# Transposing two steps in 64x64 tiles, and new instruction orders on every engine, in a fused attention and gated-MLP kernel

## The chip, the cores and the metric

The kernel runs on one core of a Trainium2 chip. The metric is device time in microseconds (us) from launch to end. The profile shows one execution: its span runs from the first to the last instruction of the program, and a little launch work lies around it.

## What is computed

Linear attention with a decay, block by block, for 4 batches, 8 heads, 768 tokens and 64 features, then a gated MLP over its output, read as 4 x 768 x 512:

```python
for b in range(nb):                                   # blocks of 64 tokens
    intra = einsum('bhic,bhjc->bhij', qb, kb) * Dmask # lam**(i-j) where i >= j
    intra = einsum('bhij,bhjd->bhid', intra, vb)
    inter = einsum('bhid,bhde->bhie', qb * lam_pow, kv_state)
    out[:, :, sl] = intra + inter
    kv_state = lam**block * kv_state + einsum('bhsd,bhse->bhde', kb * rev_pow, vb)

h = maximum(x @ w_in, 0); u, v = h[..., :512], h[..., 512:]
v_n = (v - mean(v)) / sqrt(var(v) + 1e-6)
v_s = einsum('ts,bsd->btd', w_spatial, v_n) + b_spatial[None, :, None]
return (u * v_s) @ w_out
```

## The kernel before

The tokens are worked in 12 steps of 256, three to a batch (step n belongs to batch n // 3). A step takes this way, with the name of each operation in the order table in brackets:

1. Three loads of 512 KB for q, k, v (LQ, LK, LV), each into one of three buffers, on SyncE's DMA queue (SP).
2. k times a power of lam (KM, two halves), q converted (QC) or multiplied (QM), v converted (VC), all to bf16.
3. k and q transposed. Steps 0 to 2 do it on TensorE (PE) in halves of four 128x128 transposes (TK, TQ), steps 3 and 4 with eight for k and eight for q, each set into a PSUM bank of its own; EK copies k out and EQ multiplies q by a power of lam (table `lq`, built by LT) on its way out. Steps 5 to 11 leave the transposing to the DMA (DK, DQ) and scale q before it (QM).
4. Scores (SC, 16 matmuls of 64x64 tiles, L347), masked on VectorE into `a_sb` (MK, 128x1024, L352), running state (KV, L364; KS mixes it with half the scores, L377 and L385; SS copies it out), the attention output (AV, L406 and L415), copied out as `xT` (EX).
5. The MLP's first matmuls: the v half (PV, L440) and the u half (PU, L488) with ReLU (EV, EU), statistics of v (BN, RA, RD, NB) and normalising (VN).

Once a batch's three steps are through, the spatial matmul (PW, L514, with the bias laid into PSUM before it by GP), the gate (GM), the output matmul (PO, L525; the last tile in two halves, PH, L534), its copy (EO) and the store (ST) follow, while later batches go through 1 to 5. `w_spatial` is transposed on PE first (WT, L500). The weights come by GpSimd's DMA queue, with a cast: `w_in` in two halves (WI.0 is v's, WI.1 is u's), `w_spatial` in two (WS), `w_out` (WO). GT is a 1x1 copy on GpSimd (POOL) that holds its queue until a load has landed. FN is the like on PSUM, FL four idle matmuls.

Nothing is scheduled by a planner at build time. The table `ORDER` names every operation, its step, half and PSUM banks, and the engine that runs it (last letter: T TensorE, D VectorE (DVE), A ScalarE (ACT), P GpSimd, S SyncE), and each engine runs its operations in the table's order, waiting by semaphores for its inputs and for the buffers and PSUM banks that it overwrites:

```python
for token in ORDER.split():
    name, *args, e = token.split(".")
    ops[name](e, *map(int, args))
```

Of the kernel before, what the change touches and what calls it, by code (L numbers as in the profile page):

```python
# [21 lines left out]
FL.4.6.T MK.0.0.2.3.D TQ.2.0.2.T MK.1.1.0.1.D AV.0.0.3.6.T FN.0.3.6.A TQ.2.1.0.T SS.0.1.A MK.1.0.4.5.D LT.2.A
KM.2.0.P KV.1.0.T AV.1.0.1.4.T KM.2.1.D WS.1.P TK.2.0.5.T AV.0.1.3.6.T LV.2.S SS.1.0.D FN.1.1.4.A KV.1.1.T
LK.3.S EX.0.1.6.A AV.1.1.1.4.T BS.S LK.5.S EX.1.0.1.A EK.2.0.5.D LQ.3.S EX.0.0.3.D PV.0.1.5.T FL.15.6.T
EX.1.1.4.A WO.P TK.2.1.3.T GT.1.2.P PV.1.1.1.T EV.1.1.1.A EQ.2.1.0.D EQ.2.0.2.D VC.2.P WT.0.0.0.T EK.2.1.3.D
SC.2.0.2.3.T PV.1.0.4.T BN.1.1.D PV.0.0.6.T EW.0.0.0.A MK.2.0.2.3.D EV.0.1.5.A EV.1.0.4.A SC.2.1.0.1.T SS.1.1.A
PU.1.1.5.T BN.1.0.D WT.2.0.4.T KV.2.0.T MK.2.1.0.1.D RA.1.A BN.0.1.D LV.3.S AV.2.0.2.3.T EV.0.0.6.D SS.2.0.A
FN.2.2.3.D PU.1.0.0.T BN.0.0.D AV.2.1.2.3.T EX.2.1.3.D RD.1.D WT.1.0.1.T RA.0.A NB.1.D RD.0.D EX.2.0.2.A
EW.1.0.1.D EW.2.0.4.A NB.0.D VN.0.0.A WT.1.1.6.T GT.2.1.P KM.3.0.P EW.1.1.6.D KM.3.1.P GT.2.2.P VC.3.P
WT.2.1.3.T EW.2.1.3.D PV.2.1.2.T PV.2.0.1.T VN.1.0.A PU.2.1.4.T EU.1.0.0.A VN.0.1.D LK.4.S LQ.4.S KM.4.1.P  # L30
KM.4.0.P EV.2.0.1.A QC.4.2.P PU.0.0.6.T LV.4.S PU.0.1.3.T LQ.5.S WT.0.1.0.T LV.5.S LK.6.S VN.1.1.A PU.2.0.1.T
EU.1.1.5.A EV.2.1.2.D BN.2.1.D BN.2.0.D RA.2.A RD.2.D EU.0.0.6.A GP.0.2.1.2.A EW.0.1.0.D VN.2.1.D GP.0.0.0.5.A
VN.2.0.D EU.0.1.3.A QC.3.2.D LQ.6.S GP.0.1.1.6.A EU.2.0.1.D TK.3.2.0.T PW.0.0.0.5.T GM.0.0.0.5.D EU.2.1.4.D
GP.0.2.0.3.A PW.0.2.0.3.T TQ.3.2.1.T EQ.3.2.1.D GM.0.2.0.3.D EK.3.2.0.A PW.0.2.1.2.T SC.3.1.4.5.T MK.3.1.4.5.D
KS.3.0.0.1.T SS.3.0.A GP.0.0.1.3.A PW.0.1.1.6.T GP.0.3.1.4.A KS.3.1.0.1.T KM.5.1.P KM.5.0.P DK.5.S GM.0.2.1.2.D
MK.3.0.0.1.D TK.4.2.5.T EK.4.2.5.A PW.0.0.1.3.T PW.0.3.1.4.T GP.0.1.0.2.A GM.0.1.1.6.D GP.0.3.0.0.D AV.3.0.1.5.T
# [551 lines left out]
```

## Time and profile before

| | before |
|---|---|
| median of 3 runs | 147.1 us (146.69 to 147.25) |
| the profiled execution | 147.07 us |
| its span | 145.4 us |
| PE busy | 131.9 us, 91% of the span |
| DVE, ACT, POOL busy | 113.0, 76.2, 53.7 us |
| DMA | 32.28 MB, 222 GB/s on the mean |

A busy PE is not one at its peak: matmuls are pipelined and the ends in the profile are modelled, so the distance from one group's start to the next one's tells more than the busy time. The rows quoted in the prediction give for each group its start and its length in us, and, in square brackets, how long its engine sat idle before it and what ended that.

### The profile page before, as it was taken

To read this page: it belongs to the slowest core of one execution; us is meant where nothing else is said; L and a number is where in the kernel's file an instruction comes from. 1 tells how busy PE (TensorE), PEld (TensorE's weight loads), DVE (VectorE), ACT (ScalarE), POOL (GpSimd) and SP (SyncE) were. 2 spreads that over 40 slices of the span, in tenths; PEclk is the share of its full clock that TensorE was granted. 3 is DMA by queue.
4 is the path that set the end of the run, shared out by engine and by line. 5 is a ranking of instruction groups with operands and counts; after the bars stand their busy time and mean duration, and the time that the engine had idled before them with its cause. 6 is when DMAs were issued, how large, how long until landed. Compare 5 with 4: busy or idle time off the path is not lost.

```text
span 145.4 us, 4626 instructions
## 1 busy us (share of the span) xinstructions
PE 131.9 (91%) x1954; PEld 83.2 (57%) x1954; DVE 113.0 (78%) x229; ACT 76.2 (52%) x155; POOL 53.7 (37%) x66
## 2 busy tenths in 40 slices
PE   1169989799999999999999999999999999999980
PEld 1047755578756565468565645775566556665540
DVE  2568985988898888979989889878988798972720
ACT  3775276669834224299942444594341447880250
POOL 7439920305089637672825729234000000000000
PEclk9999999999999999999999999999999999999998
DMA  3999999999999999999997998999490700082064
GB/s 83 347 347 347 229 214 216 216 230 341 302 307 301 293 118 272 239 253 333 194 312 194 284 304 194 343 207 194 147 338 19 281 12 0 5 326 107 0 265 170
DMA packets 58375, 32.28 MB, mean 222 GB/s; under 512 B 15858, under 2 KB 55282, under 8 KB 58354
## 3 DMA queue, kind: packets, MB, share of 16 engines
q1 hardware_dynamic: 55968, 29.23, 77.8%
q0 software_dynamic: 2384, 2.75, 10.8%
q8 instruction: 15, 0.25, 0.7%
q14 instruction: 6, 0.05, 0.3%
q10 hardware_dynamic: 2, 0.00, 0.0%
HBM read 24.77 MB, written 6.29 MB: 214 GB/s over the span
## 4 chain that ended last, share of the span: by engine, by line
PE 77%; DMA 12%; SPq 5%; POOL 2%; DVE 1%; issue 0%; POOLq 0%
PE ps L514 21%; PE ps L488 15%; PE ps L525 14%; PE ps L440 12%; DMA win_sb<-in_moe_w_in_dram 8%; SPq L192 5%; DMA q_in<-in_q_dram 4%; PE ps L415 3%; PE ps L406 2%; PE ps L347 2%; PE ps L316 1%; POOL kc L286 1%; PE ps L500 1%; PE ps L385 1%; PE ps L377 1%; PE ps L534 1%
## 5 line engine op out<-in xcount | busy, mean ns | idle before, releaser
L514 PE MATMUL ps<-wt_sb,vn 128*128 128x384 bf16 x192 | 34.3, 326 | 0.0
L352 DVE TENSOR_TENSOR a_sb<-ps,m 128x1024 bf16<-128x1024 f32 x24 | 28.7, 1217 | 4.3 <-PE ps L347 1.8
L286 POOL TENSOR_TENSOR kc<-k_in,lv 128x512 bf16<-128x512 f32 x20 | 20.5, 1042 | 25.0 <-DMA k_in<-in_k_dram 15.8
L488 PE MATMUL ps<-xT,win_sb 128*128 128x256 bf16 x192 | 24.0, 273 | 0.8 <-DMA win_sb<-in_moe_w_in_dram 0.8
L514 PEld LDWEIGHTS <-vn 128*128 128x128 bf16 x192 | 17.9, 98 | 11.6
L440 PE MATMUL ps<-win_sb,xT 128*128 128x512 bf16 x96 | 23.6, 380 | 0.1
L525 PE MATMUL ps<-wout_sb,gT 128*128 128x512 bf16 x92 | 22.7, 380 | 0.0
L488 PEld LDWEIGHTS <-win_sb 128*128 128x128 bf16 x192 | 18.3, 98 | 5.8 <-DMA win_sb<-in_moe_w_in_dram 1.0
L520 DVE TENSOR_TENSOR gT<-ps,uT 128x384 bf16<-128x384 f32 x32 | 16.9, 548 | 4.7 <-PE ps L514 4.6
L455 DVE BATCH_NORM_STATS2 st<-vh 128x6 f32<-128x512 bf16 x24 | 16.3, 681 | 1.5 <-ACT vh L445 1.3
L177 ACT ACTIVATE o_sb<-ps 128x512 f32<-128x512 f32 (+1 forms) x19 | 10.8, 580 | 12.1 <-PE ps L525 12.1
L445 ACT ACTIVATE vh<-ps 128x512 bf16<-128x512 f32 x17 | 10.0, 596 | 13.1 <-PE ps L440 10.7
L177 ACT ACTIVATE xT<-ps 128x512 bf16<-128x512 f32 x15 | 8.6, 596 | 14.2 <-PE ps L415 14.2
L181 POOL CAST vb<-v_in 128x1024 bf16<-128x1024 f32 x9 | 9.3, 1037 | 15.2 <-DMA v_in<-in_v_dram 11.3
L286 POOL TENSOR_TENSOR qc<-q_in,lqn 128x512 bf16<-128x512 f32 x12 | 12.5, 1049 | 4.5 <-DMA q_in<-in_q_dram 4.4
L440 PEld LDWEIGHTS <-xT 128*128 128x128 bf16 x96 | 8.6, 98 | 9.0 <-ACT xT L177 0.3
L525 PEld LDWEIGHTS <-gT 128*128 128x128 bf16 x92 | 8.5, 98 | 8.3
L177 ACT ACTIVATE ps<-bsp 128x384 f32<-128x384 f32 x21 | 10.0, 492 | 3.2 <-DVE a_sb L352 1.9
L415 PE MATMUL ps<-a_sb,vb 64*64 64x128 bf16 x384 | 10.2, 221 | 0.3 <-issue 0.3
L476 ACT ACTIVATE vn<-vh,shift,rstd 128x512 bf16<-128x512 bf16 x12 | 9.3, 806 | 0.2 <-DVE shift L470 0.2
L445 ACT ACTIVATE uT<-ps 128x512 bf16<-128x512 f32 x15 | 8.8, 590 | 1.0 <-PE ps L488 0.9
L347 PE MATMUL ps<-qT,kT 64*64 64x128 bf16 x288 | 7.9, 238 | 0.9 <-ACT kT L177 0.5
(76 smaller groups left out, 170.9 us busy)
## 6 DMA issues: line engine op xcount, KB each, us to landing
q_in<-in_q_dram SPq DMA_DIRECT2D x12, 512.0 KB, 6.2
k_in<-in_k_dram SPq DMA_DIRECT2D x12, 512.0 KB, 6.2
v_in<-in_v_dram SPq DMA_DIRECT2D x12, 512.0 KB, 6.0
out_dram<-o_sb SPq DMA_DIRECT2D x23, 256.0 KB, 2.9
wsp_raw<-in_moe_w_spatial_dram POOLq DMA_DIRECT2D x2, 576.0 KB, 12.4
win_sb<-in_moe_w_in_dram POOLq DMA_DIRECT2D x2, 512.0 KB, 10.6
wout_sb<-in_moe_w_out_dram POOLq DMA_DIRECT2D x1, 512.0 KB, 17.3
bsp<-in_moe_b_spatial_dram SPq DMA_DIRECT2D x1, 384.0 KB, 21.0
```

What stands on the lines that cost most here:

```text
L177: nc.scalar.activation(out=o, in_=i, func=AF.Copy)
L286: vec(e).tensor_tensor(out=dst[n % NCA][:, u].rearrange("p u m o d -> p o (u m) d"), in0=src[n % NIN].rearrange("p (o u) m d -> p o u m d" ...
L347: nc.tensor.matmul(out=pa[o][row(c), w, j], lhsT=kT[n % NTR][row(o), u, j, c * Q64:(c + 1) * Q64], rhs=qv(n, o, u, c), start=(w == 0 and j ...
L352: nc.vector.tensor_tensor(out=a_sb[n % NA][:, i].rearrange("p o w j x -> p o w (j x)"), in0=ps[:, b0:b1 + 1:b1 - b0].rearrange("p o (w y) ...
L415: nc.tensor.matmul(out=po[c ^ o][row(w), c, i], lhsT=vb[n % NCA][row(c), 4 * o + u, j, :], rhs=a[row(c), i, o, w, j, :], start=(r == 0 and ...
L440: nc.tensor.matmul(out=bank(b), lhsT=x[:, slot(c, g)], rhs=win_sb[:, g, DH:DFF], start=(g == 0), stop=(g == NCH - 1))
L445: nc.scalar.activation(out=o, in_=i, func=AF.Relu)
L455: nc.vector.bn_stats(out=st6[p2][:, t], in_=vh[p2][:, t])
L488: nc.tensor.matmul(out=pu[:, f2].rearrange("p (c x) -> p c x", c=2), lhsT=win_sb[:, g, f * P:(f + 1) * P], rhs=x[:, slot(0, g):slot(1, g) ...
L514: nc.tensor.matmul(out=bank(b)[:, 0:HW], lhsT=vn[bb % 2][:, s, f * P:(f + 1) * P], rhs=wt_sb[:, s, i * HW:(i + 1) * HW], start=False, stop ...
L520: nc.vector.tensor_tensor(out=gT[bb % 2][:, f, cols], in0=bank(b)[:, 0:HW], in1=uT[bb % 2][:, f, cols], op=ALU.mult)
L525: nc.tensor.matmul(out=bank(b), lhsT=gT[bb % 2][:, f, t * P:(t + 1) * P], rhs=wout_sb[:, f, :], start=(f == 0), stop=(f == NCH - 1))
```

## The change

Two things. First, steps 3 and 4 get operations of their own: TT transposes k and q together, in 128 transposes of 64x64 in place of sixteen of 128x128. Token half c goes to one of two neighbouring PSUM banks, k to the lower and q to the upper half of each bank, and FK and FQ evict k and q across the two banks at once (FK where EK was, FQ with the multiplication of EQ). Second, the whole table `ORDER` is another one: the order on every engine, the engine that some operations run on, and the PSUM banks. Counted over the table, PE's matmul operations are the same but for the two steps' transposes. Among the operations that change engine, POOL gives two casts of v to ACT and DVE and takes two multiplications of q over from DVE; DVE also hands four conversions of q and four bias copies to ACT and takes three normalisations from it.

```diff
-LQ.0.S lam.A msk.P idn.P LK.0.S LQ.1.S mkc.D QC.0.1.D posk.P pos.P LB.0.T LN.0.A LL.D QC.0.0.P LK.1.S LX.A
+lam.A LQ.1.S QC.1.0.A QC.1.1.A LK.1.S posk.P pos.P LK.0.S LQ.0.S msk.P mkc.D GT.1.1.P idn.P LB.0.T LN.0.A
...
+    def pair(b0, b1, k):
+        return ps[:, b0:b1 + 1:b1 - b0].bitcast(BF16)[:, :, 512 * k:512 * k + 512].rearrange("p c (f y) -> p c f y", y=Q64)
+
+    def both(t):
+        return t.rearrange("p u m (c y) -> p c (u m) y", c=2)
+
+    def t_t(e, n, b0, b1):
+        for k, src in enumerate((kc, qc)):
+            bk = [bank(b).bitcast(BF16)[:, 512 * k:512 * k + 512].rearrange("p (u m y) -> p u m y", u=4, m=2) for b in (b0, b1)]
+            for u in range(4):
+                for m in range(2):
+                    for o in range(2):
+                        for c in range(2):
+                            nc.tensor.transpose(out=bk[c][row(o), u, m], in_=src[n % NCA][row(c), u, m, o],
+                                                identity=ident[row(c), row(c)])
+
+    def f_k(e, n, b0, b1):
+        copy(e, both(kT[n % NTR]), pair(b0, b1, 0))
+
+    def f_q(e, n, b0, b1):
+        nc.vector.tensor_tensor(out=both(qT[n % NTR]), in0=pair(b0, b1, 1), in1=both(lq[:, n % NR]), op=ALU.mult)
...
-               SC=s_c, MK=m_k, KV=k_v, KS=k_s, SS=s_s, ...
+               SC=s_c, MK=m_k, KV=k_v, TT=t_t, FK=f_k, FQ=f_q, KS=k_s, SS=s_s, ...
```

Three places of the new orders follow. On ACT, at the start, before: `loglam` is the logarithm of lam (LN), `lqn` and `lv` are the powers for q and k (LX), `lq` the table for q after the transpose (LT).

```order
1 L196 DMA lam_in_62<-in_lam_dram 1x8
2 L210 ACT_TABLE_LOAD
3 L210 ACTIVATE loglam_64<-ps_61 128x8
4 L219 ACT_TABLE_LOAD
5 L219 ACTIVATE lqn_74<-lv_73 128x48
6 L220 ACTIVATE lv_73<-lv_73 128x48
7 L224 ACTIVATE lq_75<-posq_71,llrow_65 128x256 x8
8 L177 ACTIVATE kT_0_100<-ps_61 128x512
9 L177 ACTIVATE vb_0_98<-v_in_0_91 128x1024
```

The same place after:

```order
1 L196 DMA lam_in_62<-in_lam_dram 1x8
2 L177 ACT_TABLE_LOAD
3 L177 ACTIVATE qc_1_97<-q_in_1_86 128x2x4x64 x2
4 L210 ACT_TABLE_LOAD
5 L210 ACTIVATE loglam_64<-ps_61 128x8
6 L219 ACT_TABLE_LOAD
7 L219 ACTIVATE lqn_74<-lv_73 128x48
8 L220 ACTIVATE lv_73<-lv_73 128x48
9 L224 ACTIVATE lq_75<-posq_71,llrow_65 128x256 x4
10 L177 ACTIVATE kT_1_101<-ps_61 128x512
11 L177 ACTIVATE qc_0_96<-q_in_0_85 128x2x4x64
12 L224 ACTIVATE lq_75<-posq_71,llrow_65 128x256 x4
```

Two conversions of step 1's q now stand ahead of the logarithm, and a third table load with them; the second four `lq` pieces, which step 0 needs, stand last, behind a copy of k and another conversion.

On DVE, before, from the first mask multiplication on (`a_sb`); `xT` is the input of the first MLP matmuls:

```order
15 L352 TENSOR_TENSOR a_sb_0_104<-ps_61,m01_68 128x1024
16 L179 COPY kT_1_101<-ps_61 128x512
17 L179 CAST qc_0_96<-q_in_2_87 128x2x4x64
18 L330 TENSOR_TENSOR qT_1_103<-ps_61,lq_75 128x512
19 L352 TENSOR_TENSOR a_sb_0_104<-ps_61,m01_68 128x1024
20 L352 TENSOR_TENSOR a_sb_1_105<-ps_61,m01_68 128x1024 x2
21 L286 TENSOR_TENSOR kc_0_94<-k_in_2_90,lv_73 128x2x4x64
22 L179 CAST s_sb_2_108<-ps_61 128x256
23 L179 COPY kT_0_100<-ps_61 128x512
24 L179 CAST xT_0_110<-ps_61 128x4x128
```

The same place after (L374 is the mask multiplication there):

```order
12 L374 TENSOR_TENSOR a_sb_0_104<-ps_61,m01_68 128x1024
13 L330 TENSOR_TENSOR qT_1_103<-ps_61,lq_75 128x512 x2
14 L374 TENSOR_TENSOR a_sb_0_104<-ps_61,m01_68 128x1024
15 L374 TENSOR_TENSOR a_sb_1_105<-ps_61,m01_68 128x1024
16 L286 TENSOR_TENSOR kc_0_94<-k_in_2_90,lv_73 128x2x4x64
17 L374 TENSOR_TENSOR a_sb_1_105<-ps_61,m01_68 128x1024
18 L179 CAST xT_0_110<-ps_61 128x4x128
19 L330 TENSOR_TENSOR qT_0_102<-ps_61,lq_75 128x512
20 L179 CAST vb_0_98<-v_in_2_93 128x1024
21 L179 COPY kT_0_100<-ps_61 128x512
22 L330 TENSOR_TENSOR qT_0_102<-ps_61,lq_75 128x512
23 L179 CAST xT_1_111<-ps_61 128x4x128
```

The four masks of steps 0 and 1 are still the bulk; more of step 2's work (`qT_0`, `kT_0`, `vb_0`) now comes ahead of the `xT` that the first MLP matmul takes (step 1's, in row 23).

On POOL, before, the weight loads (DMA rows) among the first conversions:

```order
15 L181 CAST qc_0_96<-q_in_0_85 128x2x4x64
16 L286 TENSOR_TENSOR kc_1_95<-k_in_1_89,lv_73 128x2x4x64
17 L248 DMA win_sb_79<-in_moe_w_in_dram 128x4x512
18 L181 CAST qc_1_97<-q_in_1_86 128x2x4x64
19 L253 DMA wsp_raw_81<-in_moe_w_spatial_dram 128x3x768
20 L181 CAST vb_1_99<-v_in_1_92 128x1024
21 L244 COPY seen_76<-q_in_1_86 1x1
22 L181 CAST qc_0_96<-q_in_2_87 128x2x4x64
23 L248 DMA win_sb_79<-in_moe_w_in_dram 128x4x512
```

The same place after:

```order
16 L181 CAST qc_0_96<-q_in_0_85 128x2x4x64
17 L181 CAST vb_0_98<-v_in_0_91 128x1024
18 L181 CAST qc_0_96<-q_in_2_87 128x2x4x64
19 L248 DMA win_sb_79<-in_moe_w_in_dram 128x4x512
20 L181 CAST vb_1_99<-v_in_1_92 128x1024
21 L286 TENSOR_TENSOR kc_0_94<-k_in_2_90,lv_73 128x2x4x64
22 L253 DMA wsp_raw_81<-in_moe_w_spatial_dram 128x3x768
23 L248 DMA win_sb_79<-in_moe_w_in_dram 128x4x512
24 L286 TENSOR_TENSOR kc_1_95<-k_in_0_88,lv_73 128x2x4x64
```

Both halves of `w_in` now stand behind conversions of later loads (of the sixth load, q of step 2, and of the ninth, k of step 2). `w_out`, which stood three rows further down (row 26), now stands behind the second multiplication of q for step 5, ten rows further down (row 34). SyncE's queue now begins with q and k of step 1, k and q of step 0, v of step 0, q and v of step 2, v of step 1, k of step 2.

More of the change, by code (lines that the diff above doesn't have):

```diff
@@ L22 @@
[L22 to L36, printed above, removed]
@@ L82 @@
+PW.3.1.0.1.T GM.3.1.1.3.D GM.3.0.0.6.D GM.3.2.1.5.D PW.3.3.1.2.T GM.3.3.1.2.D PW.3.3.0.4.T GM.3.1.0.1.D ST.2.5.S
+PO.3.3.0.T EO.3.3.0.A ST.1.2.S PO.3.4.3.T ST.2.1.S ST.2.4.S GM.3.3.0.4.D PO.3.2.6.T EO.3.4.3.A ST.3.4.S ST.3.3.S
+EO.3.2.6.A ST.3.2.S PO.3.1.5.T EO.3.1.5.A ST.3.1.S PO.3.0.2.T EO.3.0.2.A ST.3.0.S PH.3.5.1.1.T PH.3.5.0.4.T
+EH.3.5.1.1.A SH.3.5.1.S EH.3.5.0.4.D SH.3.5.0.S
 """
```

111 lines of the change are left out of this document (61 added, 50 removed).

## The prediction

> **What bounds the kernel now.** I read the page first, then the chain that ended last, then PE's waits after 25 us.
>
> ```profile
> span 145.4 us, 4626 instructions
> PE   1169989799999999999999999999999999999980
> 14.98 11.98 DMA win_sb<-in_moe_w_in_dram
> 27.00 1.05 PE ps L488 x8
> 141.34 0.43 DVE o_sb L179
> PE ps L488 <- DMA win_sb<-in_moe_w_in_dram: 0.8, 1, 0.8
> PE ps L316 <- POOL kc L286: 0.4, 1, 0.4
> ```
>
> The second row is PE's busy share in 40 slices: it fills within some 14 us and stays at 9 to the end. The chain's rows give start and length: the second half of `w_in` lands at 14.98 + 11.98 = 26.96 us, PE takes it at 27.00, and from there PE's work follows on itself to 141.34, where the last copy and the store begin. The last two rows are all that PE waited for after 25 us. So the time is when PE reaches its dense stretch, plus its work from there, plus the gaps in it. An operation on another engine counts only where it moves one of these three. The profiled execution took 147.07 us, 1.67 beyond its span and 0.03 under the median, so I add to 147.07. About 0.5% (0.7 us) is what a measurement of this kernel can tell from no change.
>
> **The start.** Here the new order does most. ACT's timeline of before, then DVE's:
>
> ```profile
> 1.34 1.28 ACT L210 ACT_TABLE_LOAD   x1 [1.34 <-PEq L572]
> 3.56 0.18 ACT L210 ACTIVATE loglam<-ps 128x8 f32<-128x8 f32 x1 [0.94 <-PE ps L207]
> 3.76 1.28 ACT L219 ACT_TABLE_LOAD   x1
> 6.22 0.24 ACT L220 ACTIVATE lv<-lv 128x48 f32<-128x48 f32 x1
> 6.37 3.28 ACT L224 ACTIVATE lq<-posq,llrow 128x256 bf16<-128x256 f32 x8
> 9.56 0.57 ACT L177 ACTIVATE kT<-ps 128x512 bf16<-128x512 bf16 x1
> 11.01 1.06 ACT L177 ACTIVATE vb<-v_in 128x1024 bf16<-128x1024 f32 x1 [0.87 <-DMA v_in<-in_v_dram]
> ...
> 4.96 0.43 DVE L179 CAST qc<-q_in 128x512 bf16<-128x512 f32 x1 [2.08 <-DMA q_in<-in_q_dram]
> 6.52 0.69 DVE L286 TENSOR_TENSOR kc<-k_in,lv 128x512 bf16<-128x512 f32 x1 [0.35 <-ACT lv L220]
> 9.69 0.42 DVE L330 TENSOR_TENSOR qT<-ps,lq 128x512 bf16<-128x512 bf16 x1 [0.64 <-ACT lq L224]
> 11.82 0.41 DVE L330 TENSOR_TENSOR qT<-ps,lq 128x512 bf16<-128x512 bf16 x1
> 12.15 1.21 DVE L352 TENSOR_TENSOR a_sb<-ps,m 128x1024 bf16<-128x1024 f32 x1
> 14.93 3.49 DVE L352 TENSOR_TENSOR a_sb<-ps,m 128x1024 bf16<-128x1024 f32 x3
> 18.34 0.68 DVE L286 TENSOR_TENSOR kc<-k_in,lv 128x512 bf16<-128x512 f32 x1
> 20.35 0.69 DVE L179 CAST xT<-ps 128x512 bf16<-128x512 f32 x1 [0.56 <-PE ps L415]
> 20.96 0.74 DVE L330 TENSOR_TENSOR qT<-ps,lq 128x512 bf16<-128x512 bf16 x2
> ```
>
> In before both table loads of 1.28 us lie under other waits, the power table `lv` is there at 6.46, `lq` ends at 9.65, and the first mask starts at 12.15. After, ACT first converts step 1's q, which lands where before's first load did, at 4.95. The row for 1024 elements has 1.06, that for 256 has 0.41 from one to the next (3.28 over eight), so I take 0.60 for 512. ACT then goes: two conversions to 6.15; the logarithm's table load, no longer under a wait, to 7.43; the logarithm to 7.6; the load for the powers to 8.9; `lqn` and `lv` to 9.4, against 6.46. Step 1's `lq` (four pieces, 1.6) to 11.0, a kT copy 0.5, a conversion 0.6, step 0's `lq` 1.6: to 13.7, against 9.65. DVE has multiplied its four k halves by then and waits. Then two qT and one kT (0.33 each, from 11.82 to 12.15) to 14.7, and the first mask starts at **14.85, 2.7 us later** than before.
>
> From there DVE's list decides. Up to the xT for the first v matmul it has four masks at 1.14 (14.93 to 18.34 is three), four qT and a kT at 0.33, two xT and a v conversion at 0.61 (20.35 to 20.96), one k half at 0.6: 4.56 + 1.65 + 1.83 + 0.6 = 8.6, done at 23.5. In before the first v matmul comes at 20.96. But its list left 1.5 us of step 2's conversions for later, and PE then still stood 0.8 for `w_in`, so I carry the sum to the first u matmul, before's 27.00. After, PE does more ahead of it: KV of step 2, both AV of step 2, two WT and one PV:
>
> ```profile
> 20.96 1.04 PE L440 MATMUL ps<-win_sb,xT 128*128 128x512 bf16 x4
> 27.00 1.05 PE L488 MATMUL ps<-xT,win_sb 128*128 128x256 bf16 x8 [0.80 <-DMA win_sb<-in_moe_w_in_dram]
> ...
> 30.07 0.24 PE ps L406 x8
> 30.31 0.22 PE ps L415 x16
> 30.53 0.78 PE ps L500 x12
> 31.81 1.73 PE ps L440 x8
> ...
> 23.97 0.69 DVE L455 BATCH_NORM_STATS2 st<-vh 128x6 f32<-128x512 bf16 x1 [1.07 <-ACT vh L445]
> 24.80 1.19 DVE L352 TENSOR_TENSOR a_sb<-ps,m 128x1024 bf16<-128x1024 f32 x1
> ```
>
> By these rows an AV is 0.46, two WT 0.78, a PV 0.87, and a KV 0.2 (sixteen at 14 ns, below): 2.8 together, so before's equal point is 29.8. After, DVE goes on from 23.5 with a mask (1.14), an xT (0.61), a statistics pair (0.83, from 23.97 to 24.80) once PV's ReLU is through at 25.4, and a mask, to 27.4. PE then does both AV and the four idle matmuls to 28.6, three WT to 29.7 while the last xT is copied, and PV to 30.6. The first u matmul starts at 30.6, **+0.8**. It is at least about 0, where `w_in` would hold PE (below), and up to +1.2 with each of the six masks at the 1.21 of a single one. I take +1.0, between the sum and that end, since the sum lets hand-overs between engines cost nothing.
>
> **The weights.** POOL's rows and the page's row of the landing times:
>
> ```profile
> 10.63 0.93 POOL L248 DMA_DIRECT2D win_sb<-in_moe_w_in_dram  x1
> win_sb<-in_moe_w_in_dram POOLq DMA_DIRECT2D x2, 512.0 KB, 10.6
> 14.13 0.43 DVE L179 CAST qc<-q_in 128x512 bf16<-128x512 f32 x1 [0.44 <-DMA q_in<-in_q_dram]
> ```
>
> 10.6 is the middle of two, and one is 11.98, so the first half took 9.2 and landed at 19.8. After, its issue stands behind the conversion of the sixth load. The fifth landed at 11.0 (ACT's `vb` row), the seventh at 14.0, so the sixth at 12.5, the issue comes at 13.3, the landing at 22.5: in time for 23.5. The second half landed 7.1 after the first, so 29.6: in time for 30.6, by 1.0. `w_out` leaves late. POOL's second multiplication for step 5 overwrites the buffer that step 3's q is transposed from, so it waits for TT.3 (37 us by the sum above) and the issue comes at about 40.5. With the 9.2 of `w_in`'s first half it lands at 49.7, just where the first PO stands (after five more PW, TT.4 and two tile groups from 41.5). Between 0 and 1.0 of waiting; I take +0.4.
>
> **The transposes.** PE rows of a 128x128 set and of 64x64 groups:
>
> ```profile
> 39.65 0.61 PE L316 MATMUL ps<-ident,qc 128*128 128x128 bf16 x8
> 40.10 1.14 PE L514 MATMUL ps<-wt_sb,vn 128*128 128x384 bf16 x6
> 55.89 0.41 PE L364 MATMUL ps<-vb,kc 64*64 64x64 bf16 x16
> 56.38 0.64 PE L347 MATMUL ps<-qT,kT 64*64 64x128 bf16 x32
> ```
>
> A set of eight takes 0.45 from its start to the next group's, so a step's k and q 0.90. No row shows a 64x64 transpose. The nearest is L364: 64 columns moved, sixteen in 0.41 less one's own 0.19, over fifteen, 14 ns each, with two of the four tiles in use at a time. TT uses all four in turn. If four run at once as L347's do (twice the columns in the same 14 ns), 128 take 0.93; if each costs 14 ns whatever runs beside it, 1.8. I take 1.0, by L347. That is +0.1 for each of two steps, up to +0.9. Changes between 64x64 groups and full ones are as many as before, 26 from the first PW on by the two orders, so TT adds none. The evictions have the elements of before.
>
> **The dense stretch.** The matmuls are the same. Before has two gaps from PW on: ahead of step 4's k (the 0.4 that L316 waits for POOL, in the first fence) and ahead of 56.38, where the last of L364's sixteen starts at 55.89 + 0.22 = 56.11 and the score matmuls 0.27 later. I let both go, -0.7, since TT.4 now stands behind AV of step 3 and DVE hands work over. In a new order of 139 PE groups something else will be late: I put 0.5 back, an estimate by those two gaps, of 0 to 2.
>
> Sum: 147.07 + 1.0 (start) + 0.2 (TT) + 0.4 (`w_out`) - 0.7 + 0.5 (gaps) = **148.5**.
>
> **Rivals.** *The start is absorbed* (not slower). If ACT's chain is at least 0.8 shorter (the 1.28 of the table load that stands ahead of the logarithm is the one piece that a different placing could take out whole), DVE's first mask starts before 14.05, PE is ready for the u matmul before 29.6, and `w_in`'s landing decides, as in before. Then the start costs nothing, and with the gaps closed and `w_out` in time the time is 147.07 + 0.2 - 0.7 = 146.6, and 146.1 where `w_in` lands 0.5 earlier than my sum as well. For it: in before PE had time to spare there, 0.8 at `w_in`. Against it: the order puts the table load where nothing covers it. *Transposes one after another*: if tiles don't overlap in a transpose, each is half of the 56 ns of a 128-column one, 28 ns, 3.6 us a step; 147.07 + 1.0 + 5.4 + 0.2 (the other terms) = 153.7. The L364 row speaks against it. The Trainium skill ("TensorE: Matmul & The Clock Gate", Part 1) says that start-to-start never drops below about 25 ns however few the columns; by it a step would take 3.2 us, an estimate. The 14 ns of L364 and L347 in this trace are already below that floor. At 14 ns each, the milder form, the time is 148.5 + 1.6 = 150.1. *A cold PE clock*:
>
> ```profile
> 11.29 1.03 PE L316 MATMUL ps<-ident,kc 128*128 128x128 bf16 x8
> 18.93 0.40 PE L316 MATMUL ps<-ident,kc 128*128 128x128 bf16 x4
> ```
>
> Eight transposes took 1.03 at 11.29 against 0.61 at 39.65, and four took 0.40 at 18.93, so PE ran at half pace at first and at the full one by then. After, it waits for masks between 16.5 and 18 and again before 23.5; if it comes to the PVs at half pace, two of them (0.87 each at the full pace) cost 1.7 more: 150.2. The Trainium skill (the same page, "The HAM clock gate") says that the clock is released after a window of about 3.4 us of sustained work, free-running; the dense 18 to 22.5 of my sum would hold such a window, so by that rule the clock is up in time.
>
> **How the numbers follow.** Forecast case (147.6 to 149.3) 0.47; start absorbed 0.25; TT at 14 ns 0.08, one after another 0.02; cold clock 0.10; gaps or `w_out` at their upper ends (149.3 to 150.6) 0.08. A fifth of the forecast case, 0.09, lies below 147.8. Of the absorbed case 0.12 falls below 146.4 and 0.13 above it. So faster 0.12, same 0.22, slower 0.66. The range leaves out 153.7, the top of the late cases and the lowest part of the absorbed one: 146.2 to 150.3.
>
> **What would show it.** The first mask at 14 to 15 us with a third table load ahead of the logarithm at 6.2; the first v matmul at 23 to 24, the first u matmul at 30 to 31 without a wait for `w_in`; TT at 0.9 to 1.1 us to the next group; PE gaps after 40 us under 1 us together. It is wrong if the first u matmul waits for `w_in` or starts before 30, if TT takes over 1.5, or if PE shows more than 2 us of gaps from PW on.

## The result, and the profile after

The changed kernel takes 148.63 us (median of 5 runs, 148.27 to 149.37), the kernel before 147.10 beside it (146.68 to 147.80): ratio 1.0115, 95% interval 1.0069 to 1.0162. It is slower by 1.2%, clear of the noise, and the forecast was 148.5. Ratios here and below leave out slow runs, those over 1.5% above the fastest of the same kernel, and the medians don't (three of e4's six runs are slow, and one each of e9's and e11's twelve). The profiled execution took 148.52 us, 1.45 more than that of before.

The page of after: span, PE's busy share and the granted clock in 40 slices of 3.67 us.

```profile
span 146.8 us, 4817 instructions
PE   0318599999999999999999999999999999999990
PEclk9999956999999999999999999999999999999999
```

PE fills later than in before, and the granted clock (the share of PE's full clock that the chip gave it) is halved around 18 to 25 us. ACT's timeline, then DVE's:

```profile
4.72 1.15 ACT L177 ACTIVATE qc<-q_in 128x512 bf16<-128x512 f32 x2 [2.10 <-DMA q_in<-in_q_dram]
5.89 1.28 ACT L210 ACT_TABLE_LOAD   x1
7.38 1.28 ACT L219 ACT_TABLE_LOAD   x1
8.95 0.24 ACT L220 ACTIVATE lv<-lv 128x48 f32<-128x48 f32 x1
...
15.11 1.22 DVE L374 TENSOR_TENSOR a_sb<-ps,m 128x1024 bf16<-128x1024 f32 x1
20.40 1.23 DVE L374 TENSOR_TENSOR a_sb<-ps,m 128x1024 bf16<-128x1024 f32 x1 [0.55 <-PE ps L369]
22.47 0.68 DVE L179 CAST vb<-v_in 128x1024 bf16<-128x1024 f32 x1
23.82 0.42 DVE L330 TENSOR_TENSOR qT<-ps,lq 128x512 bf16<-128x512 bf16 x1 [0.33 <-PE ps L316]
24.60 0.69 DVE L179 CAST xT<-ps 128x512 bf16<-128x512 f32 x1 [0.35 <-PE ps L437]
```

The third table load is there, ahead of the logarithm and under nothing. The power table is ready at 9.19 against 6.46, the first mask starts at 15.11 against 12.15. Between it and the `xT` for the first v matmul DVE stands three times, each time for PE. PE's timeline:

```profile
18.18 0.64 PE L437 MATMUL ps<-a_sb,vb 64*64 64x128 bf16 x16 [1.04 <-DVE a_sb L374]
25.35 1.90 PE L462 MATMUL ps<-win_sb,xT 128*128 128x512 bf16 x8 [0.22 <-DVE xT L179]
32.49 1.92 PE L510 MATMUL ps<-xT,win_sb 128*128 128x256 bf16 x16
38.11 0.45 PE L347 MATMUL ps<-ident,kc 64*64 64x64 bf16 x32
38.39 0.43 PE L347 MATMUL ps<-ident,qc 64*64 64x64 bf16 x32
38.76 1.92 PE L510 MATMUL ps<-xT,win_sb 128*128 128x256 bf16 x16
40.51 1.79 PE L536 MATMUL ps<-wt_sb,vn 128*128 128x384 bf16 x10
```

The first u matmul stands at 32.49, against before's equal point of 29.8: +2.7. The first w_spatial matmul stands at 40.51. Before's is at 37.65 with 0.45 of step 3's transposes still to come, so its equal point is 38.1: +2.4. PE's waits after 25 us and the last row of the chain:

```profile
PE ps L437 <- DVE a_sb L374: 0.2, 1, 0.2
PE ps L462 <- DVE xT L179: 0.2, 1, 0.2
143.25 0.42 DVE o_sb L179
```

The last copy starts at 143.25 against 141.34: +1.9, so the stretch from the first w_spatial matmul on became 0.5 shorter. From there to the end of the span it is 3.55 against 4.03, another 0.5 back. In sum +2.7 (start), -0.3 (to the first w_spatial matmul), -0.5 (dense stretch), -0.5 (tail): 1.4 of the 1.45.

### The profile page after: what moved, and what is told of

Read it like the earlier page. It is cut to its first block, busy times and chain, and to the rows that moved or that the text cites. A ratio compares the mean times of both kernels' runs of the same rounds, so it can differ in the third digit from the quotient of the medians.

```text
span 146.8 us, 4817 instructions
## 1 busy us (share of the span) xinstructions
PE 131.4 (89%) x2050; PEld 83.2 (57%) x2050; DVE 108.6 (74%) x217; ACT 82.5 (56%) x166; POOL 52.5 (36%) x65
## 4 chain that ended last, share of the span: by engine, by line
PE 57%; DMA 12%; DVE 8%; ACT 6%; SPq 5%; POOL 4%; issue 3%; POOLq 0%; DVEq 0%
PE ps L536 12%; PE ps L462 11%; PE ps L547 11%; PE ps L510 8%; DMA k_in<-in_k_dram 5%; DMA v_in<-in_v_dram 5%; PE ps L437 4%; DVE a_sb L374 3%; POOL qc L286 3%; PE ps L316 3%; DMA q_in<-in_q_dram 3%; PE ps L428 2%; DVE kc L286 2%; SPq L303 2%; SPq L192 2%
## 5 line engine op out<-in xcount | busy, mean ns | idle before, releaser
L536 PE MATMUL ps<-wt_sb,vn 128*128 128x384 bf16 x192 | 34.8, 326 | 0.1
L374 DVE TENSOR_TENSOR a_sb<-ps,m 128x1024 bf16<-128x1024 f32 x24 | 28.7, 1217 | 2.6 <-PE ps L399 1.2
L286 POOL TENSOR_TENSOR kc<-k_in,lv 128x512 bf16<-128x512 f32 x19 | 19.5, 1045 | 19.6 <-PE ps L399 14.1
L286 POOL TENSOR_TENSOR qc<-q_in,lqn 128x512 bf16<-128x512 f32 x14 | 14.4, 1043 | 21.2 <-PE ps L347 11.6
L177 ACT ACTIVATE xT<-ps 128x512 bf16<-128x512 f32 x16 | 9.2, 598 | 13.4 <-PE ps L437 13.4
L177 ACT ACTIVATE o_sb<-ps 128x512 f32<-128x512 f32 (+1 forms) x18 | 10.2, 584 | 10.3 <-PE ps L547 10.3
L177 ACT ACTIVATE ps<-bsp 128x384 f32<-128x384 f32 x25 | 12.2, 493 | 5.9 <-DVE gT L542 2.9
L467 ACT ACTIVATE vh<-ps 128x512 bf16<-128x512 f32 x18 | 10.6, 591 | 5.5 <-PE ps L462 5.5
L177 ACT ACTIVATE s_sb<-ps 128x256 bf16<-128x256 f32 x15 | 5.7, 383 | 10.5 <-PE ps L386 5.6
L179 DVE COPY o_sb<-ps 128x512 f32<-128x512 f32 (+1 forms) x7 | 4.4, 646 | 6.8 <-PE ps L556 4.6
L437 PEld LDWEIGHTS <-vb 64*64 64x64 bf16 x384 | 7.9, 117 | 2.3 <-issue 2.3
```

The lines of the kernel that those rows point to most:

```text
L177: nc.scalar.activation(out=o, in_=i, func=AF.Copy)
L286: vec(e).tensor_tensor(out=dst[n % NCA][:, u].rearrange("p u m o d -> p o (u m) d"), in0=src[n % NIN].rearrange("p (o u) m d -> p o u m d" ...
L374: nc.vector.tensor_tensor(out=a_sb[n % NA][:, i].rearrange("p o w j x -> p o w (j x)"), in0=ps[:, b0:b1 + 1:b1 - b0].rearrange("p o (w y) ...
L437: nc.tensor.matmul(out=po[c ^ o][row(w), c, i], lhsT=vb[n % NCA][row(c), 4 * o + u, j, :], rhs=a[row(c), i, o, w, j, :], start=(r == 0 and ...
L467: nc.scalar.activation(out=o, in_=i, func=AF.Relu)
L536: nc.tensor.matmul(out=bank(b)[:, 0:HW], lhsT=vn[bb % 2][:, s, f * P:(f + 1) * P], rhs=wt_sb[:, s, i * HW:(i + 1) * HW], start=False, stop ...
```

## The experiments

The question was what makes up the 2.7 us of the start, and what the 64x64 form is worth without the new orders. All ratios are to the kernel before on the same chip, in us the times of five landmarks in the profiled execution of each:

| run | median | ratio [95%] | first mask | first v | first u | first w_spatial | last copy |
|---|---|---|---|---|---|---|---|
| before | 146.7 to 147.1 | 1 | 12.15 | 20.96 | 27.00 | 37.65 | 141.34 |
| after | 148.63 | 1.0115 [1.0069, 1.0162] | 15.11 | 25.35 | 32.49 | 40.51 | 143.25 |
| e7, before, copy first | 148.86 | 1.0146 [1.0106, 1.0186] | 13.98 | 23.39 | 28.80 | 40.89 | 144.05 |
| e1, logarithm first | 148.02 | 1.0082 [1.0053, 1.0111] | 13.98 | 23.35 | 31.84 | 39.90 | 142.82 |
| e2, w_in earlier | 148.10 | 1.0090 [1.0056, 1.0124] | 15.47 | 25.39 | 32.53 | 40.39 | 142.91 |
| e8, weights early | 147.22 | 1.0029 [1.0003, 1.0054] | 13.97 | 23.48 | 30.62 | 38.47 | 142.30 |
| e13, last version | 147.22 | 1.0014 [0.9988, 1.0040] | 13.97 | 24.21 | 31.35 | 39.21 | 141.91 |
| e11 | 147.44 | 1.0036 [1.0009, 1.0063] | 13.97 | 23.67 | 30.82 | 38.67 | 142.07 |
| e3, idle matmuls | 150.56 | 1.0255 [1.0228, 1.0283] | 15.55 | 26.31 | 33.69 | 41.54 | 145.42 |
| e4, all three | 150.19 | 1.0147 [1.0085, 1.0208] | 13.97 | 25.51 | 32.65 | 40.50 | 144.58 |
| e9, weights and clock | 147.68 | 1.0032 [0.9995, 1.0070] | 13.96 | 23.65 | 30.79 | 38.65 | 143.08 |
| e12, w_in and clock | 148.11 | 1.0071 [1.0037, 1.0106] | 15.73 | 25.18 | 32.32 | 40.17 | 142.69 |
| e5, full transposes | 149.02 | 1.0149 [1.0117, 1.0181] | 15.62 | 25.40 | 32.73 | 40.97 | 143.67 |
| e6, before with 64x64 | 148.89 | 1.0141 [1.0110, 1.0172] | 11.97 | 21.02 | 27.17 | 37.53 | 143.12 |

### The table load, put into before (e7) and taken out of after (e1)

```diff
 # e7, before
-LQ.0.S lam.A msk.P idn.P LK.0.S LQ.1.S mkc.D QC.0.1.D posk.P
+LQ.0.S lam.A QC.0.1.A msk.P idn.P LK.0.S LQ.1.S mkc.D posk.P
 # e1, after
-lam.A LQ.1.S QC.1.0.A QC.1.1.A LK.1.S ... FL.0.1.T LX.A KM.1.0.D
+lam.A LQ.1.S LK.1.S ... FL.0.1.T LX.A QC.1.0.A QC.1.1.A KM.1.0.D
```

> The kernel before, where one copy of q on ACT is put ahead of the logarithm (QC.0.1 goes from DVE to ACT there), so that ACT loads a table set three times at the start instead of twice: the mirror of the run with the logarithm first. Theory 1 (a Copy ahead of the logarithm costs one more table load of 1.28 us, and the loss comes through the first decay products): first mask 1.3 to 2.2 us later than 12.15 us, first v matmul at 22.2 to 23.0 instead of 20.96; w_in's wait of 0.80 us takes up its part, so 147.2 to 148.2 us, ratio 1.003 to 1.010. Theory 2 (the start has slack, the third load is hidden behind the first loads of q and k): 146.7 us, ratio within 0.002 of 1.

ACT's timeline of e7, with the first mask behind it:

```profile
4.75 0.63 ACT L177 ACTIVATE qc<-q_in 128x512 bf16<-128x512 f32 x1 [2.13 <-DMA q_in<-in_q_dram]
5.39 1.28 ACT L210 ACT_TABLE_LOAD   x1
6.88 1.28 ACT L219 ACT_TABLE_LOAD   x1
8.45 0.24 ACT L220 ACTIVATE lv<-lv 128x48 f32<-128x48 f32 x1
...
13.98 1.21 DVE L352 TENSOR_TENSOR a_sb<-ps,m 128x1024 bf16<-128x1024 f32 x1
```

One copy moved ahead of the logarithm, and the power table is 2.2 us later, the first mask 1.8, the first v matmul 2.4. Not all of the 2.2 is the load: the copy waits for its q until 4.75, and the logarithm stands behind it. Without the load at 5.39 the power table would be there at 7.4, so about 1.3 is the load and 0.9 the copy's place, an estimate from these rows. The mechanism is theory 1; the size is over its range (1.003 to 1.010), at 1.0146: the wait for `w_in` (0.80) took only part of it, the first u matmul being 1.8 later. The profiled execution was 0.9 us over its median, so its later landmarks overstate the loss. The Trainium skill ("ScalarE: Activation LUTs", section "Table sets: the hidden batching unit") says that tables are loaded as sets, and that calls are to be batched by set. The rows agree in that each change of set costs a load, and they add that the set loaded for a plain copy in front didn't serve the logarithm. They differ in one point: the page counts a logarithm followed by an exponential as one load, and here each has its own (5.39 and 6.88).

> After, with step 1's two q conversions on ACT moved behind the logarithm and the powers, so that the third table load goes. If the table load delays the start (my theory): lv ready about 1.6 us earlier (7.6 for 9.2), the first mask at 13.6 to 13.9 for 15.1, the first half of w_in issued about 1.3 earlier (it waits behind TQ of step 0), the first u matmul at 31 for 32.5, the time 1.2 to 1.6 below after's, that is a ratio to before of 1.000 to 1.003. If PE's half clock alone sets the stretch from the first mask to the u matmul: the first mask moves, but the half clock stays up to the same window's end and the time falls by under 0.5, a ratio above 1.007.

The other way round, the first v matmul came 2.0 us earlier, as theory 1 says, but the time fell by only 0.6 where theory 1 had 1.2 to 1.6. PE's timeline of e1, then a row of its chain, then DVE's and ACT's first rows:

```profile
31.84 1.92 PE L510 MATMUL ps<-xT,win_sb 128*128 128x256 bf16 x16 [1.18 <-DMA win_sb<-in_moe_w_in_dram]
...
18.79 13.00 DMA win_sb<-in_moe_w_in_dram
...
4.15 0.46 DVE L239 COPY m<-mfull 64x256 bf16<-64x256 bf16 x2 [4.15 <-POOL mfull L233]
5.54 0.18 ACT L210 ACTIVATE loglam<-ps 128x8 f32<-128x8 f32 x1 [2.91 <-PE ps L207]
```

PE is ready at 30.66 and stands 1.18 for the second half of `w_in`, which lands at 31.79; `w_out`, which lands at 50.55, holds it for another 0.36 until 50.59. In the changed kernel neither wait shows: there both halves land (25.13 and 32.45) just as the late PE arrives. A limit that costs nothing in one trace is the next one in line.

The last two rows show one more. With the third load gone the power table is there at 7.55, still 1.1 later than in before, and the first mask 1.8 later. In the new order POOL makes the positions ahead of the mask, so DVE's copy of the mask waits until 4.15 (2.07 in before). DVE fills `one_row` only behind it, and PE's matmul of lam with `one_row` (L207) and then the logarithm start at 4.91 and 5.54, against 2.93 and 3.56. In after this lies under ACT's copies and the third load. No run moves it back, so what it costs was not measured.

### The weights (e2, e8)

```diff
 # e2, after
-MK.0.1.2.3.D QC.2.0.P EQ.1.1.4.D ... SC.0.0.0.1.T WI.0.P KV.0.1.T
+MK.0.1.2.3.D WI.0.P QC.2.0.P EQ.1.1.4.D ... SC.0.0.0.1.T KV.0.1.T
 # e8: e1, and
-MK.0.1.2.3.D QC.2.0.P ... WI.0.P KV.0.1.T ... WI.1.P KM.3.0.P GT.1.2.P GT.2.1.P WS.1.P ... QM.5.1.P ... WO.P
+MK.0.1.2.3.D WI.0.P QC.2.0.P ... WI.1.P KV.0.1.T ... WS.1.P KM.3.0.P GT.1.2.P GT.2.1.P ... WO.P QM.5.1.P
```

> After, with the first w_in load issued ahead of the conversion of step 2's q, at 11.9 for 15.1. If w_in is the only late one: it lands at 22 to 23 for 25.1, the first v matmul moves to about 24 and the first u matmul by 1 us or more, ratio to before 1.004 or less. If xT is as late by itself (half clock, late first mask): the first v matmul stays at 25.2 to 25.4, the u matmul at 32.3 to 32.5, and the time within 0.3 of after's, ratio 1.009 to 1.013.

The first half landed at 20.01, five us early, and the first v matmul stayed at 25.39: `w_in` was not what held the changed kernel's start. Its median is 0.5 us under after's, but the intervals overlap.

> The changed kernel with the logarithm ahead of step 1's two ACT copies (as in the run with the logarithm first) and all four later weight loads issued earlier: w_in's first half ahead of step 2's q copy, its second half in the place of the first, w_spatial's second half ahead of step 3's K products, w_out ahead of step 5's q products. Theory 1 (the new order of the start costs through the third ACT table load and then through weights that land just in time, one after the other: 25.13, 32.45, 36.09 us): first v matmul at 23.3, first u matmul at 30.5 instead of 32.49, first w_spatial matmul at 38.5 instead of 40.51, the whole 146.4 to 147 us, ratio 0.997 to 1.002. Theory 2 (the weights' landing is set by the loads that share the DMA engines, so an earlier issue pushes q, k and v back): v matmul or w_spatial matmuls wait for q, k or v, first w_spatial matmul not before 39.5, 147.7 us or more, ratio over 1.006.

With the logarithm first and the weights early, the start gains what theory 1 says: first v matmul 23.48, first u 30.62, first w_spatial 38.47, and 147.22 us, just over its range. So most of the loss is in ACT's copies with their table load and then in the weights, which follow one another as limits. What is left shows in PE's timeline and in the chain of e8:

```profile
45.93 0.45 PE L347 MATMUL ps<-ident,qc 64*64 64x64 bf16 x32 [1.05 <-POOL qc L181]
...
34.12 10.60 DMA q_in<-in_q_dram
```

The q load of step 4 lies beside the early `w_out`, takes 10.60 us (the median of the q loads is 6.1), and the second set of 64x64 transposes waits for its conversion.

### The clock (e3, e4, e12, e9)

The windows of after, cut where the granted clock changes, then a set of four transposes in before (columns of the windows: stretch, its length, busy time of PE, PEld, DVE, ACT, POOL, granted clock, DMA share, GB/s):

```profile
14.46:17.87 3.41, 1.99 (x84) 1.57 (x84) 3.41 (x6) 1.26 (x3) 3.34 (x4) 1.00 1.15 347
17.87:24.70 6.83, 6.52 (x168) 5.64 (x169) 5.59 (x10) 3.21 (x10) 3.31 (x7) 0.50 1.16 265
...
17.34 0.58 PE L316 MATMUL ps<-ident,qc 128*128 128x128 bf16 x4
```

After a stretch of 3.41 us in which PE was busy for 1.99, the clock stood at half for 6.83 us, though PE was busy for 6.52 of them. Before was not at the full clock all along either. The trace's first record of its clock starts at 17.93, and the profile counts the time ahead of a first record as full; but PE's rows have half pace until then, 0.58 for four transposes at 17.34 against 0.40 at 18.93. (In after the first record starts at 14.46, and the same holds.) So from the first mask to the first v matmul PE was at half for 6.8 of 10.2 us in after and for 5.8 of 8.8 in before. What does the half clock cost there?

```diff
 # e3, after: idle matmuls of 128 columns, 28 more
-SC.1.1.2.3.T MK.0.0.0.1.D AV.0.0.4.5.T
+FL.0.5.T FL.0.5.T SC.1.1.2.3.T MK.0.0.0.1.D FL.0.5.T FL.0.5.T FL.0.5.T FL.0.5.T FL.0.5.T AV.0.0.4.5.T
 # e4: e1 + e2 + e3
 # e12: e2, and the four of the start moved, 256 columns wide (e9: e8, and the same with 512)
-QC.0.0.P LL.D FL.0.1.T LX.A ... MK.0.0.0.1.D AV.0.0.4.5.T
+QC.0.0.P LL.D LX.A ... MK.0.0.0.1.D FL.0.5.T AV.0.0.4.5.T
```

> After, with 28 more idle matmuls (seven groups of four) in PE's waits of 16.2 to 18.2, to keep the clock up. If PE's activity decides the clock: no half clock from 17.9 to 24.7, the first xT ends at 23.6 to 24.2 for 25.3, but the first half of w_in, still landing at about 25.1, holds the first v matmul, so the time falls by 0.3 at most: ratio 1.008 to 1.012, with less spread between runs. If the clock has nothing to do with these waits: the half clock comes as before and the first xT stays at 25.3.

It got 1.9 us slower than after, which neither theory has. Two rows of PE in e3:

```profile
22.35 0.56 PE L316 MATMUL ps<-ident,kc 128*128 128x128 bf16 x7 [1.74 <-issue]
49.14 0.22 PE L347 MATMUL ps<-ident,qc 64*64 64x64 bf16 x3 [1.13 <-issue]
```

PE stood twice for nothing that the profile shows, in the middle of a set of transposes, 2.9 us together. Up to the first of these waits the clock was full, from 16.00 on, as the first theory has it; it was at half from 22.83 to 26.24, after a stretch of 3.41 us with PE busy for 1.68. What the full clock is worth can't be read from this run.

> After with the three edits of the others together (logarithm first, w_in earlier, idle matmuls). If table load, clock and w_in each hold the start by themselves: first mask at 13.7, first v matmul at 22 to 23, first u matmul at 29 to 30 for 32.5, the time 2.5 to 3.3 below after's, ratio to before 0.988 to 0.995, more than the three gains alone add up to. If something later holds the dense stretch anyway: less than 1 us below after's, ratio above 1.004.

Missed by far, 150.19 against 146. Its runs spread from 147.65 to 152.34. In the profiled one PE was still at half pace (its first record of the full clock starts at 19.14), so the 20 idle matmuls ahead of the first masked product took 2.3 us: it started at 19.19, where e1 has 17.05, and DVE then stood 1.70 for PE. The profiled one also has another such wait, of 1.46 us at 48.43, and a conversion of v on DVE that took 1.54 instead of 0.68 and held the scores of step 2 for 1.48. I can't say what stretched it. The sum of the three gains was not tested.

> The changed kernel with w_in's first half ahead of step 2's q copy (as in the run with w_in earlier, where it landed at 20.01 us, long before the first v matmul at 25.39), and with the four idle matmuls of the start moved into PE's wait ahead of the first masked product, 256 columns wide: 0.43 us together at the full clock and 0.95 at half, so they fit into that wait of 1.04 us in either case, and the number of PE instructions stays as it is. Theory 1 (the half clock between mask and xT costs the 1.4 us by which this stretch is longer than before's): full clock through 18 to 25 us, first v matmul at 24.0 to 24.6, first u matmul then at w_in's second half, about 31.9. Theory 2 (DVE's own list sets the pace there, the half clock only hides behind it): the first v matmul moves by less than 0.5 us, to 24.9 to 25.4, and the whole stays at 147.9 to 148.4 us.

With the number of PE instructions kept, no such wait came. PE's rows:

```profile
17.91 1.04 PE L268 MATMUL ps<-ident 128*128 128x256 bf16 x4
24.57 0.42 PE L373 MATMUL ps<-qT,kT 64*64 64x128 bf16 x16 [0.47 <-DVE qT L334]
```

The clock was full from 22.4 us instead of 24.0 in e2, and the first v matmul moved by 0.2: PE now waits for DVE's `qT`. The numbers are those of theory 2, but the full clock through 18 to 25 us, which theory 1 supposes, did not come about.

> The same as the kernel with the weights early, and besides the four idle matmuls of the start are moved to the place ahead of the first masked product, each 512 columns wide instead of 128, so that the number of PE instructions stays as it is while PE is busy through its wait for the mask. Theory 1 (the half clock after that wait costs 0.8 to 1.2 us of the start): the granted clock stays full from 14 us on, first v matmul at 22.3 to 22.7, first u matmul at 29.4 to 30.0, the whole 0.5 to 1 us under the kernel with the weights early. Theory 2 (the clock follows from the whole start's small waits, or DVE sets the pace of the start in any case): first v matmul stays at 23.2 to 23.6 and the time changes by less than 0.3 us.

Full clock from 18.5, first v matmul at 23.65, no earlier than e8's 23.48: near theory 2's numbers. But the idle matmuls came while the clock was still half and put the first masked product 0.9 us back, and DVE stood 0.86 for PE, so this run doesn't separate the theories either. A cleaner pair came by itself. Up to the first v matmul e8 and e13 have the same orders; the clock became full at 21.43 in the one and at 23.32 in the other. A set of four transposes in each and DVE's last two operations ahead of the first v matmul, e8 first:

```profile
21.77 0.40 PE L316 MATMUL ps<-ident,qc 128*128 128x128 bf16 x4
22.27 0.42 DVE L330 TENSOR_TENSOR qT<-ps,lq 128x512 bf16<-128x512 bf16 x1
22.73 0.69 DVE L179 CAST xT<-ps 128x512 bf16<-128x512 f32 x1
...
21.97 0.61 PE L316 MATMUL ps<-ident,qc 128*128 128x128 bf16 x4
22.68 0.42 DVE L330 TENSOR_TENSOR qT<-ps,lq 128x512 bf16<-128x512 bf16 x1 [0.33 <-PE ps L316]
23.46 0.69 DVE L179 CAST xT<-ps 128x512 bf16<-128x512 f32 x1 [0.35 <-PE ps L437]
```

Up to 22 us DVE's lists agree to 0.02 us; then it waits for PE twice in e13, 0.68 together, and the first v matmuls are at 23.48 and 24.21. After has the same two waits, and one of 0.55 at 20.40. That one is missing in e5 (below), which has after's orders up to here and the full clock from 16.08 to 19.49 and again from 22.90: from the first mask to the start of this `xT` it takes 8.50 us there and 9.49 in after. So the half clock costs 0.7 to 1.0 us between runs of equal orders, by when it comes, and by these rows up to the 1.23 of DVE's three waits; without them DVE's list takes 9.0. These pairs differ in their clock by themselves, and no run holds it full through the whole stretch.

### The 64x64 form (e5, e6)

```diff
 # e5, after
-TT.3.0.1.T ... FK.3.0.1.A ... FQ.3.0.1.D ... TT.4.4.5.T ... FK.4.4.5.D FQ.4.4.5.D
+TK.3.2.0.T TQ.3.2.1.T ... EK.3.2.0.A ... EQ.3.2.1.D ... TK.4.2.4.T TQ.4.2.5.T ... EK.4.2.4.D EQ.4.2.5.D
 # e6, before
-TK.3.2.0.T PW.0.0.0.5.T ... TQ.3.2.1.T EQ.3.2.1.D ... EK.3.2.0.A ... TK.4.2.5.T EK.4.2.5.A ... TQ.4.2.6.T SS.3.1.A ... EQ.4.2.6.D
+PW.0.0.0.5.T ... TT.3.0.1.T FQ.3.0.1.D ... FK.3.0.1.A ... TT.4.3.6.T SS.3.1.A FK.4.3.6.A ... FQ.4.3.6.D
```

> The changed kernel with the 64x64 transposes of steps 3 and 4 put back to 16 transposes of 128x128 a step and the two copies of before; all orders stay as changed. Theory 1 (the 64x64 form saves PE about 0.25 us a step, as its slot of 0.65 us in the changed trace stands to 0.90 us for the two full-width slots before): first w_spatial matmul at about 40.75 us, where the changed kernel has 40.51, the dense stretch ends 0.5 us later, 149.1 us, ratio to the kernel before about 1.015. Theory 2 (the 64x64 form costs PE 0.1 us a step, as the prediction had it): 148.4 us, ratio about 1.010. Theory 3 (it is neutral, PE waits for something else there): 148.6 us.

149.02 us, first w_spatial matmul at 40.97, last copy 0.4 later: theory 1. Half of the 0.46 at the first w_spatial matmul is the slot (0.90 from step 3's k to the next group, 38.33 to 39.23, against 0.65), the rest a start that was 0.2 later in this execution (`w_in` held its first v matmul for 0.59). The difference of the medians, 0.39, is within the intervals; the slot is not in doubt. That it reaches the end is not shown: from the first w_spatial matmul to the last copy e5 takes 102.7 us, as after does, with the full transposes of step 4 in it.

> The kernel before, with its own orders, where only the transposes of steps 3 and 4 become 64x64 tiles into two banks with one copy each for K and for q; the 64x64 transposes stand where the q transposes stood. Theory 1 (the form saves 0.25 us a step and all the loss is in the new orders): 146.3 to 146.7 us, ratio 0.994 to 0.997. Theory 2 (the form itself costs, by its wait for both K and q before either is transposed, or by 0.1 us of PE a step): 147.3 to 148 us, ratio 1.001 to 1.006.

Theory 1 falls, and the loss of 2.2 us is beyond theory 2's range (0.6 to 1.3). PE's waits of e6 after 37 us, then the copies of step 3 and a gate multiplication (GM) in e6, then the copies of step 3 in after:

```profile
PE ps L369 <- ACT kT L177: 0.8, 1, 0.8
PE ps L407 <- DVE qT L354: 0.8, 1, 0.8
PE ps L347 <- DVE gT L542: 0.3, 1, 0.3
...
40.68 0.69 DVE L354 TENSOR_TENSOR qT<-ps,lq 128x1024 bf16<-128x1024 bf16 x1
41.41 1.02 ACT L177 ACTIVATE kT<-ps 128x1024 bf16<-128x1024 bf16 x1 [2.62 <-DVE qT L354]
49.18 0.56 DVE L542 TENSOR_TENSOR gT<-ps,uT 128x384 bf16<-128x384 f32 x1 [1.88 <-ACT kT L177]
...
39.73 1.00 ACT L177 ACTIVATE kT<-ps 128x1024 bf16<-128x1024 bf16 x1
40.77 0.69 DVE L354 TENSOR_TENSOR qT<-ps,lq 128x1024 bf16<-128x1024 bf16 x1 [1.72 <-ACT kT L177]
```

With k and q in the same two banks, their copies run one behind the other, in both kernels: the one that stands first in the table is waited for. In before k's copy has two w_spatial groups' time before q is transposed; with TT both start where q's did, and the scores come 0.8 us before k is there, in step 4 the state group 0.8 before q. The third wait, 0.3, is that of step 4's transposes for a bank that a gate multiplication still reads. Part of this can be e6's choice of banks, 3 and 6 for step 4, where after has neighbouring ones: DVE's multiplication from bank 4 waited 1.88 us for the copy of k out of these two, and q's own then 0.82 for masked products of step 3, which go to banks 1 and 5. No run separates the banks from the form. In after's order TT stands four PE groups ahead of the scores that use it, and that hides the pair. The form saves PE 0.25 us a step and needs an order that gives its copies the time.

### What was left (e11, e13)

```diff
 # both: e8 with WO at its place in after, and
-AV.3.0.0.1.T FN.3.0.1.D TT.4.4.5.T GP.0.0.1.2.A PW.0.3.1.6.T SS.3.1.D
+AV.3.0.0.1.T FN.3.0.1.D GP.0.0.1.2.A PW.0.3.1.6.T TT.4.4.5.T SS.3.1.D
 # e11: VC.2.D becomes VC.2.P, behind WS.1; e13 instead:
-GP.0.3.1.6.D
+GP.0.3.1.6.A
```

> The changed kernel with the logarithm first and w_in's and w_spatial's loads early, as in the run with the weights early, but w_out left at its own place, so that it no longer lies beside the q load of step 4 (on which the second group of 64x64 transposes waited 1.05 us there); besides, these transposes stand one w_spatial group later, and step 2's v copy goes from DVE (0.68 us between two masks) to POOL. Theory 1 (what was left of the loss lies in these two waits): first v matmul at 22.8 to 23.4, first w_spatial matmul at 37.9 to 38.4, no wait at the second 64x64 transposes, the whole 145.4 to 146.4 us, ratio 0.991 to 0.998. Theory 2 (the loads of q, k and v are late as a whole by then, and the wait moves to the next load): 146.6 to 147.3 us, ratio 0.999 to 1.004.

In e11 the conversion of step 2's v comes after the state that should use it, which takes step 0's v in its place, so only its waits are of use here. No wait at the transposes any more, but 0.52 for the bias copy on DVE ahead of the w_spatial group that went first, and the conversion, queued on POOL, freed nothing: the first v matmul stayed at 23.67. Theory 2.

> The changed kernel with the logarithm first and w_in and w_spatial early; w_out at its own place; the second group of 64x64 transposes one w_spatial group later, and the bias copy that PE waited for there (0.52 us, on DVE behind two masks) on ACT. Nothing else is moved. Theory 1 (the two waits of 1.05 and 0.52 us are what kept the dense stretch at 103.8 us instead of the 102.7 of the changed kernel): first w_spatial matmul at 38.5, PE's end at 141.2 to 141.6, 146.1 to 146.7 us, ratio 0.994 to 0.999. Theory 2 (a third wait follows): 147 us or more, ratio 1.001 to 1.005.

From the first w_spatial matmul to the last copy it is 102.7 us, as in after and 0.5 under before's 103.2, and no third wait shows, which is theory 1. But the start was 0.7 behind e8's, as this execution's clock came late, and the time, 147.22 us, ratio 1.0014 [0.9988, 1.0040], is theory 2's: no difference from before. Whether the other eleven runs lose it at the start too isn't known. It takes back the loss of the change. None of the versions beats the kernel before.

## Why the prediction was right

The number was right, and the mechanism that it put first, the third table load with ACT's copies ahead of the logarithm, is the one that e7 shows. But that the sum came out is luck: its largest term, the start, was 1.7 us too low, more than twice the 0.7 that can be told from no change here, and the others were as much too high. Of its signs the mask (0.1 late) and the small gaps came; the first v matmul, the first u matmul and the slot of TT were all outside.

- **The table load and the first mask**: right. Third load at 5.89 (foretold 6.15), power table 9.19 (9.4), first mask 15.11 (14.85). The late `one_row` is not in the sum; in after it lies under the rest.
- **From the mask to the first v matmul**: foretold 8.6, measured 10.2. DVE's operations took 9.0, 0.4 more than their rows said; the step that failed is the one that I named, "the sum lets hand-overs between engines cost nothing". DVE waited three times for PE, 1.23 us together, and the pairs above show each of these waits gone where PE had the full clock. With +0.3 from the mask this makes the first u matmul 32.49 instead of 30.6, and the start +2.7 instead of +1.0: the mis-sized term.
- **The cold clock**: I made it a case of its own with 0.10 and had it hit the v matmuls, which ran at full pace (25.35 to 27.2). It came in the stretch before them, where it accounts for up to 1.2 of the 1.6 us above. The rule of the Trainium skill that I cited ("TensorE: Matmul & The Clock Gate", "The HAM clock gate"), clock up after a window of sustained work, agrees with the trace. Of the two windows of 3.41 us at half, PE stood idle in the first until 18.18; it was busy through the second, and at its end, 24.70, the clock was full. What failed is my use of it: a free-running window of 3.41 us need not lie whole within 18 to 22.5.
- **`w_in`**: I missed a wait. The conversion ahead of its issue on POOL writes the buffer from which step 0's q is transposed:

```profile
14.53 0.62 POOL L181 CAST qc<-q_in 128x512 bf16<-128x512 f32 x1 [2.69 <-PE ps L316]
```

So the issue came at 15.09 (foretold 13.3) and the halves landed at 25.13 and 32.45 (22.5 and 29.6). It cost nothing only because the start was late too; in e5, whose `xT` was there earlier, it held PE for 0.59.
- **The start is absorbed** (0.25): it needed ACT's chain 0.8 shorter. e1 made it 1.6 shorter (power table at 7.55), and `w_in` did become the limit, as that rival says; with the true landing this gives 148.02, not 146.6.
- **The transposes**: I miscounted. The loop makes 64 transposes of 64x64 a step, k and q together (128 is the count of both steps; the text on the change has it wrong as well). The pace taken from L347 was near: 7.3 ns each, 0.93 us for 128, and measured 8.8 ns, 32 in 0.28 us (38.11 to 38.39). So it is 0.65 a step against 0.90, where the forecast had +0.1. Sign wrong, by the count. e5 agrees on the slot. One after another at 28 ns, or 14 each, is out.
- **`w_out`**: issued at 41.97, 8.3 us to land, first use at 50.79: 0 instead of +0.4, where the range began.
- **The gaps**: -0.7 + 0.5 was forecast; what is left in after is 0.2 ahead of AV of step 3. The dense stretch is 0.5 shorter. The transposes of step 4 aren't shown to be the reason, since e5 has the same 102.7 with the full ones; before's wait of 0.4 for POOL, which is gone, is of that size. The tail is another 0.5 shorter, of which I said nothing: it is 3.5 to 3.6 in every version with the new orders and 4.0 in those with the old, and why was not looked into.

The forecast sum was 1.0 + 0.2 + 0.4 - 0.2 = +1.4; the measured one is +2.7 - 0.3 - 0.5 - 0.5 = +1.4. A start 1.7 worse was paid for by three smaller terms, each better than forecast.

## What to carry to other kernels

Look at what ACT does first: a plain copy ahead of the first table function makes that function wait for the copy's input and brought a table load of its own, here about 2 us of a 147 us kernel for both. And look at how long the engines wait for each other while PE's clock is at half: here that was the term that a sum of operation times missed. When such a start is repaired, repair the transfers that were timed to it as well; they are the next limit, and the gain stays with them until they move. Before pricing a new operation by its rows, count its loop once more.
